# A windowed attention with a routed mixture of experts: root, scatters and copies in another order

## The chip, the cores and the metric

The kernel runs on one core of one Trainium2 chip. The metric is device time in microseconds (us). An execution that the hardware profiler recorded gives the profile page and the trace; three other executions give the median.

The engines of the core are named as the profile names them: PE is TensorE (PEld are its weight loads), DVE is VectorE, ACT is ScalarE, POOL is GpSimd, and SP is SyncE, which only issues transfers here.

## The reference

The inputs are q, k, v of shape (4, 8, 768, 64), eight expert vectors, and the two weight arrays of eight experts. All is float32.

```python
scores = scale * np.matmul(q, k.transpose(0, 1, 3, 2))
is_global = pos[None, :] < n_global                      # 8
is_local = (rel >= 0) & (rel < n_local)                  # 96
scores = np.where(keep, scores + bias, -1e9)             # bias: -slope of the head * distance
a = softmax(scores)
x = (a @ v) laid out as (3072, 512)

xn = x / (norm(x) + 1e-6);  en = expert_emb / (norm(expert_emb) + 1e-6)
logits = xn @ en.T / tau
expert_idx = np.argmax(logits, axis=1)
gate_w = softmax(logits)[arange(N), expert_idx]
for e in range(E):                                       # 8 experts, 512 -> 1024 -> 512
    h = np.maximum(x[mask] @ w1[e], 0.0)
    out[mask] = gate_w[mask, None] * (h @ w2[e])
```

## The kernel before

**The two stages.** The first stage (window_attention) computes attention and decides for each of the 3072 tokens which expert takes it. It writes the token's row to x_dram, and for each token a small record (its number twice and its gate) into a slot of its expert's list, meta, in device memory. The second stage reads the lists back, gathers each expert's rows, multiplies them by the expert's two weight matrices, and scatters the results to the output.

**The steps of the first stage.** A step handles two blocks of 96 queries, for four heads. A batch has two groups of heads (m = 0 and 1) and four steps (p) in each group, so there are 32 steps; in the last batch the two groups' steps are interleaved by halves. In step s TensorE first computes the scores of that step (score, L480: 64 short matmuls), then some transposes of coming queries and keys (turn, L455), then the router's matmuls and transposes for halves of a batch that are ready, and then the values' products of the step before (attend, L509 and L519). ScalarE takes the exponential of the scores (grow, L486) and VectorE multiplies it by a table of window and slope (weigh, L493). At every second step attend ends with copies out of PSUM: two xd copies (L524 on ScalarE; L525 on VectorE, from step 22 on ScalarE) and a copy or addition of the denominators, den (L530, L532, VectorE).

**The PSUM banks.** Five banks pa0 to pa4 go round for scores, transposes and router products. A bank is taken again when its reader (an exponential, a copy, a product) is done. Three further banks, od, hold the values' products; they are taken again once xd and den have been copied out.

**The router.** When a half of a batch (384 tokens) has its attention output, an object hf goes through phases, one a step: turn_x and store_x (L582, L591: the product of x with the reciprocal denominators, its store to x_dram, and on ScalarE its sum of squares, L596), turn_sums (L550, L553), score_experts (L559), turn_products (L568 to L574). Then the generator choose makes the decision, for a whole batch in the first two batches and for half a batch in the others. There are thus six routers. Its pieces, separated by yield, are: largest logit and one-hot choice (L203 to L211); the running counts by matmuls (L217, L220) and, on POOL, the root of the sums of squares (L224, a power of one half); adding the counts (L228, L230); then one piece with the reciprocal root and its product with the logits (L234, L235, L236, VectorE), the gate's exponential (L237, ScalarE), the slot number and the gate's sum (L240 to L250, VectorE). The last piece puts six or three scatters on a list, k.later.

**The scatters.** One scatter takes 128 tokens. VectorE writes the reciprocal gate into the record mt (L256), and POOL issues an indirect DMA of 128 records of 12 bytes to meta (L257). scatter_later takes the first one, two or three of the list in a step (one before step 24, two before step 29, three from there on), and makes each wait for the last score matmul of that step (scored). It stands before the router's turns of the step; in a step in which a router's phase equals hf.count, it stands behind them (L790 and L810).

**What sets the order.** On TensorE, ScalarE, VectorE and SP the order of the first stage is the order in which the program is written. POOL's order is chosen by the scheduler from what each instruction depends on. POOL has three kinds of work in the steps: copies of the values' first rows (v, L430), the roots (L224), and the scatters (L257). Late in the stage it also gathers the rows of expert 0's first 256 slots (first_gathers, L991), once these have been read back (L981). TensorE's products of those rows (first_turn, first_product, L663 and L671) follow the last step and stand beside the last router, its scatters, and the read of all lists (L1676).

**What calls the pieces.** half_turns sends the router on at phases 1 and hf.count; the loop's own lines send it on once more before attend; half_router, behind attend, sends it on to the large last piece when the phase is over hf.count. So the whole of L234 to L250 stands behind attend and its copies.

Of the kernel before, what the change touches and what calls it, by code (L numbers as in the profile page):

```python
# [12 lines left out]
ALU = mybir.AluOpType  # L13
# [178 lines left out]
def choose(k, b, i0, n, lg, ss, pool):  # L192


    nc, E = k.nc, k.E
    sl = slice(i0, i0 + n)
    lg, ss, eidx = lg[:, sl, :], ss[:, sl], k.eidx[:, 0:n, :]
# [23 lines left out]
                         rhs=oh[:, t : t + 1, :].to_broadcast([P, n - t, E]), start=False, stop=True,  # L221
                         skip_group_check=True)

    nc.gpsimd.tensor_tensor(out=ss, in0=ss, in1=k.half[:, 0:n], op=ALU.pow)  # L224

    yield
    both = new([n + 1, E], "both")
# [6 lines left out]
    nc.vector.tensor_scalar_add(ss, ss, 1e-6)  # L234
    nc.vector.reciprocal(out=ss, in_=ss)  # L235
    nc.vector.tensor_tensor(out=lg, in0=lg, in1=ss.unsqueeze(2).broadcast_to([P, n, E]), op=ALU.mult)  # L236
    nc.scalar.activation(lg, lg, AF.Exp)  # L237

    within = both[:, 0:n, :]
# [14 lines left out]
    def scatter(t, behind):  # L254

        nc.vector.reciprocal(out=mt[:, t : t + 1, 2], in_=gate[:, t : t + 1])  # L256
        i = nc.gpsimd.indirect_dma_start(  # L257
            out=k.meta[:], out_offset=bass.IndirectOffsetOnAxis(ap=slot[:, t : t + 1], axis=0),
            in_=mt[:, t, :], in_offset=None,
        )  # L260
        if behind:
            wait_for(k, i, [behind])

        if k.scatters:
            k.tc.declare_no_dep(i.ins, group="scatters", reason="slots are distinct")
        k.tc.add_to_no_dep_group("scatters", i.ins)
        k.scatters.append(i.ins)
# [28 lines left out]
def scatter_later(k, n, behind=None):  # L296

    for scatter, t in k.later[:n]:
        scatter(t, behind)
    del k.later[:n]  # L300


def route(k, b, xb, pool):

    nc, NT, E = k.nc, k.NT, k.E
    ss = pool.tile([P, NT], F32, name="ss", tag="ss")
    for t in range(NT):
        sq = pool.tile([P, k.DM], F32, name="sq", tag="sq")
        nc.scalar.activation(sq[:], xb[:, t, :], AF.Square, accum_out=ss[:, t : t + 1])
    lg = pool.tile([P, NT, E], F32, name="lg", tag="lg")  # L310
    for t in range(NT):
        tp = k.work.tile([P, 512], F32, name="work", tag="work")
        for c in range(k.NC):
            nc.tensor.transpose(tp[:, c * P : (c + 1) * P], xb[:, t, c * P : (c + 1) * P], k.ident[:])
        xt = pool.tile([P, k.NC, P], F32, name="xt", tag="xt")
        nc.scalar.copy(out=xt[:].rearrange("p c n -> p (c n)"), in_=tp[:])
        lp = k.work.tile([P, 512], F32, name="work", tag="work")
        for c in range(k.NC):
            nc.tensor.matmul(lp[:, 0:E], lhsT=xt[:, c, :], rhs=k.en[:, c, :],
                             start=c == 0, stop=c == k.NC - 1)  # L320
        nc.vector.tensor_copy(out=lg[:, t, :], in_=lp[:, 0:E])
    steps = choose(k, b, 0, NT, lg, ss, pool)
    next(steps)
    steps.send(k.work.tile([P, 512], F32, name="work", tag="work"))
    next(steps)
    next(steps)

# [49 lines left out]
def window_attention(k, ctx):  # L377
# [25 lines left out]
    def bank():  # L403
        turn_of[0] += 1
        return banks[turn_of[0] % len(banks)]
# [191 lines left out]

    def start_half(t, h):
        hf = Net()
        hf.t, hf.h, hf.phase = t, h, 0  # L600
        late = t.b >= B - 2

        hf.count = 2 if late else 3
        hf.router = choose(k, t.b, 3 * h if late else 0, 3 if late else NT, t.lg, t.ss, rt_p) if late or h else None
        return hf
# [10 lines left out]
    def half_turns(hf):  # L616
# [12 lines left out]
        if hf.router and hf.phase == hf.count:  # L629
            hf.router.send(k.free)  # L630

    def half_router(hf):

        if hf.router and hf.phase > hf.count:
            next(hf.router)
        if hf.phase == hf.count + 1 and hf.h == 1 and hf.t.b < B - 2:
            check_sums(hf.t)
        if (hf.t.b, hf.h, hf.phase) == (B - 2, 1, 3):
            first_base()
# [110 lines left out]
        for s, x in zip(at, pieces):  # L750
            turns[s].append(x)

    waiting, active = [], []
    weights = [(0, i) for i in range(PIECES)]
    for s, (g, p) in enumerate(steps):
        if s % 8 == 0:
# [29 lines left out]
        grow(us[0], 0)  # L786
        grow(us[0], 1)
        weigh(us[0])
        due = 1 if s < len(steps) - 8 else 2 if s < len(steps) - 3 else 3
        if not any(hf.router and hf.phase == hf.count for hf in active):  # L790
            scatter_later(k, due, scored)
            due = 0
        grow(us[1], 0)
        todo = [(x.pairs[a], i) for x, a, i in turns[s]]
        if todo:
# [11 lines left out]
            weigh(us[1])  # L807
        for hf in active:
            half_turns(hf)
        scatter_later(k, due, scored)  # L810
        if s == len(steps) - 1:
            first_gathers()
        ready = s > 8 * (B - 1) - 2 and steps[s - 1][0].m == 1 and steps[s - 1][1] % 2
# [3 lines left out]
        for hf in active:  # L817
            if hf.router and hf.phase == hf.count:
                next(hf.router)
        if s > 0:  # L820
            q, qp = steps[s - 1]
            attend(q, qp, s < len(steps) - 10)
            if q.m == 1 and qp % 2:
                waiting.append((prev, qp // 2))
# [20 lines left out]
    hf = start_half(t, 1)  # L845
# [11 lines left out]
    k.weights = weights  # L857
    first_product(0)
    hf.router.send(bank()[:, 3 * P :])
    next(hf.router)  # L860
    next(hf.router)
    scatter_later(k, len(k.later))
# [403 lines left out]
def wait_for(k, i, others):  # L1266
    for x in others:
        k.tc.add_manual_dep(i.ins, x.name,
                            mybir.DependencyInfo(mybir.DependencyClass.Sync, mybir.DependencyReason.DATA),
                            reason="it comes behind all of them")  # L1270
# [509 lines left out]
```

## Time and profile before

| | us |
|---|---|
| three executions | 522.73, 523.97, 524.47 (median 523.97) |
| the profiled execution | 524.56 |
| its span, first to last instruction | 522.8 |
| TensorE busy | 500.1 (96%) |
| VectorE busy | 301.8 (58%) |
| ScalarE busy | 197.2 (38%) |
| POOL busy | 153.7 (29%) |
| indirect DMA of a scatter (L257), on POOL, mean, 24 of them | 1.13 |
| v copy (L430), mean, 15 of them | 1.24 |
| root (L224), median of six | 0.89 |
| L234, L236, L237, median | 0.16, 0.18, 0.22 |

A matmul's end is modelled, so a busy TensorE need not be one at its peak. Idle time of an engine that is not on the way to the end costs nothing. In a row of the timeline the figure in brackets is the time that the engine stood idle before it, and what ended that time; "issue" is time in which it waited for nothing that the profile shows.

### The profile page before, as it was taken

The numbers are of one execution on the slowest core, as the hardware profiler recorded it, in microseconds if no ns is written. First come the engines' busy times: TensorE is split into PE (matmuls) and PEld (weight loads), VectorE is DVE, ScalarE is ACT, GpSimd is POOL, SyncE is SP. The second block draws the span as 40 slices with busy tenths as digits, with TensorE's granted clock in tenths as the row PEclk, the third lists the DMA queues.
The fourth block names the chain that finished last, engine by engine and source line by source line (L and its number), as shares of the span: only waits on it lengthen the run. The fifth ranks groups of instructions, "written<-read, shape, count | busy, mean of one in ns | idle before, by whom it ended". The sixth has DMA issues, their size and how long they took to land.

```text
span 522.8 us, 13699 instructions
## 1 busy us (share of the span) xinstructions
PE 500.1 (96%) x5606; PEld 411.3 (79%) x5606; DVE 301.8 (58%) x602; ACT 197.2 (38%) x493; POOL 153.7 (29%) x169
## 2 busy tenths in 40 slices
PE   7899999999988998999999999999999999999995
PEld 7677887887765787859878759989889789859964
DVE  5647667666685664756745606765646644715531
ACT  4867766766653411302322312412312222302210
POOL 4221121442544235354240024144053050013023
PEclk9999999999998999999999999999999999999999
DMA  9999998898443346817573018357056064001001
GB/s 169 200 188 181 220 261 207 212 229 177 104 103 92 94 102 118 265 56 287 195 284 118 2 44 296 150 197 263 3 217 242 4 224 163 1 16 67 0 22 67
DMA packets 111421, 76.32 MB, mean 146 GB/s; under 512 B 87077, under 2 KB 95269, under 8 KB 111281
## 3 DMA queue, kind: packets, MB, share of 16 engines
q1 hardware_dynamic: 102769, 59.00, 42.1%
q0 software_dynamic: 6912, 15.26, 8.8%
q8 instruction: 63, 1.03, 0.9%
q14 instruction: 77, 0.63, 0.4%
q10 hardware_dynamic: 1600, 0.39, 0.3%
HBM read 61.66 MB, written 17.16 MB: 151 GB/s over the span
## 4 chain that ended last, share of the span: by engine, by line
PE 67%; issue 18%; DVE 3%; POOL 3%; ACT 3%; DMA 3%; SPq 1%; POOLq 1%; ACTq 0%; DVEq 0%
PE big L1303 17%; PE big L1108 9%; PE od L509 7%; PE pa L480 5%; PE work L1236 4%; PE od L519 3%; PE pa L455 3%; PE work L1108 3%; PE work L1249 3%; PE pa L671 2%; PE work L1017 2%; POOL out_dram L1255 2%; PE big L1279 2%; PE pa L582 2%; PE work L1027 1%
## 5 line engine op out<-in xcount | busy, mean ns | idle before, releaser
L493 DVE TENSOR_TENSOR ex<-ex,table 126x768 f32<-126x768 f32 x64 | 61.3, 964 | 45.1 <-ACT ex L486 44.9
L1315 DVE TENSOR_TENSOR hT<-big,hT 128x320 f32<-128x320 f32 (+4 forms) x70 | 39.4, 566 | 49.9 <-PE big L1303 49.7
L1255 POOL DMA_INDIRECT out_dram<-y_arm,tids x17 | 17.1, 1004 | 167.4 <-ACT y_arm L1238 121.1
L486 ACT ACTIVATE ex<-pa 126x384 f32<-126x384 f32 (+1 forms) x128 | 53.3, 477 | 24.4 <-PE pa L480 18.6
L1303 PE MATMUL big<-xT,w1t 128*128 128x160 f32 (+4 forms) x336 | 59.4, 330 | 1.1 <-issue 1.1
L1303 PEld LDWEIGHTS big<-xT,w1t 128*128 128x128 f32 x336 | 54.2, 190 | 3.9 <-issue 2.0
L991 POOL DMA_INDIRECT xg<-x_dram,idss x32 | 35.4, 1106 | 42.9 <-PE big L1303 21.5
L509 PE MATMUL od<-ex,v 126*64 126x192 f32 (+1 forms) x576 | 47.0, 309 | 0.0
L480 PE MATMUL pa<-qT,kT 64*32 64x128 f32 (+4 forms) x2048 | 41.0, 263 | 3.7 <-issue 3.5
L480 PEld LDWEIGHTS pa<-qT,kT 64*32 64x32 f32 (+1 forms) x2048 | 30.2, 105 | 16.7 <-issue 12.3
L257 POOL DMA_INDIRECT meta<-mt,slot x24 | 27.2, 1133 | 49.9 <-DVE rd L553 20.9
L509 PEld LDWEIGHTS od<-ex,v 126*64 126x64 f32 x576 | 35.3, 139 | 7.9 <-issue 3.8
L1303 PE MATMUL big<-xsum,fsum 128*128 128x160 f32 (+4 forms) x224 | 39.6, 330 | 0.0
L1020 ACT COPY xT<-work 128x256 f32<-128x256 f32 x56 | 18.1, 375 | 56.0 <-PE work L1017 55.3
L1303 PEld LDWEIGHTS big<-xsum,fsum 128*128 128x128 f32 x224 | 36.1, 190 | 1.2
L1236 PE MATMUL work<-w2t,hT 128*128 128x512 f32 x80 | 35.1, 594 | 0.0
L1108 PE MATMUL big<-wsum,hsum 128*128 128x256 f32 x136 | 31.1, 380 | 1.1 <-issue 0.6
L1317 ACT ACTIVATE hT<-hT 128x320 f32<-128x320 f32 (+4 forms) x42 | 21.6, 533 | 25.5 <-DVE hT L1315 25.3
L430 POOL COPY v<-v 30x896 f32<-30x896 f32 (+1 forms) x15 | 18.4, 1239 | 41.1 <-DMA v<-in_v_dram 28.9
L1108 PEld LDWEIGHTS big<-wsum,hsum 128*128 128x128 f32 x136 | 25.7, 190 | 5.6 <-issue 1.4
L1236 PEld LDWEIGHTS work<-w2t,hT 128*128 128x128 f32 x80 | 15.1, 190 | 17.7 <-issue 17.6
L1113 DVE TENSOR_TENSOR ptmp<-big,ptmp 128x256 f32<-128x256 f32 x16 | 6.7, 421 | 38.0 <-PE big L1108 20.0
(246 smaller groups left out, 899.8 us busy)
## 6 DMA issues: line engine op xcount, KB each, us to landing
w1t<-in_moe_w_dram SPq DMA_DIRECT2D x6, 2048.0 KB
w2t<-in_moe_w_dram SPq DMA_DIRECT2D x6, 2048.0 KB
v<-in_v_dram SPq DMA_DIRECT2D x32, 192.0 KB
x_dram<-xs SPq DMA_DIRECT2D x23, 256.0 KB
k<-in_k_dram SPq DMA_DIRECT2D x28, 192.0 KB
q<-in_q_dram SPq DMA_DIRECT2D x28, 192.0 KB
w1t<-in_moe_w_dram SPq DMA_DIRECT2D x32, 128.0 KB
w2t<-in_moe_w_dram SPq DMA_DIRECT2D x32, 128.0 KB
```

What stands on the lines that cost most here:

```text
L257: i = nc.gpsimd.indirect_dma_start(out=k.meta[:], out_offset=bass.IndirectOffsetOnAxis(ap=slot[:, t : t + 1], axis=0), in_=mt[:, t, :], in ...
L480: i = nc.tensor.matmul(u.sp[e][k0:k1, a * n + c0 : a * n + c1], lhsT=t.kT[rows, j, k0:k1], rhs=t.qT[rows, j * BLK + c0 : j * BLK + c1], st ...
L486: nc.scalar.activation(u.ex[:, e], u.sp[e][0:ROWS, 0 : 2 * u.n].rearrange("p (a c) -> p a c", a=2), AF.Exp, scale=k.scale)
L493: nc.vector.tensor_tensor(out=exv, in0=exv, in1=tab[:, :, 0 : u.n // BLK, :], op=ALU.mult)
L509: nc.tensor.matmul(g.od[a][e * D : (e + 1) * D, at : at + c1 - c0], lhsT=g.v[0:ROWS, 2 * a + e, u.j, :], rhs=u.ex[:, e, a, c0:c1], start=f ...
L991: i = k.nc.gpsimd.indirect_dma_start(out=xg[:], out_offset=None, in_=k.x_dram[0 : upto or k.N + 1, :], in_offset=bass.IndirectOffsetOnAxis ...
L1108: i = self.k.nc.tensor.matmul(ps, lhsT=x[:, f, :], rhs=w[:, f, :], start=f == 0 and not add, stop=True, skip_group_check=True)
L1236: nc.tensor.matmul(ps[:], lhsT=hT[:, f, j * P : (j + 1) * P], rhs=w2[:, f, :], start=i == 0, stop=i == k.NF - 1)
L1255: i = k.nc.gpsimd.indirect_dma_start(out=k.out.rearrange("t (i m) -> (t i) m", i=n), out_offset=bass.IndirectOffsetOnAxis(ap=ids, axis=0), ...
L1303: nc.tensor.matmul(to[f // 2][:, f % 2 * 256 : f % 2 * 256 + h], lhsT=x[:, l, f * P : (f + 1) * P], rhs=y[:, l, 0:h], start=not (add or f ...
L1315: nc.vector.tensor_tensor(out=to, in0=x, in1=z, op=ALU.add)
L1317: nc.scalar.activation(to, to, AF.Relu)
```

## The change

1. choose keeps its root instruction in k.root, and scatter_later makes every scatter that it issues in a step wait for that root as well as for scored.
2. scatter_later stands in one place in every step, before the second unit's exponentials and the router's turns; the second place and its condition are gone.
3. The router's last piece is cut in two by a yield behind L236. A new function half_root sends the router through the first part (L234 to L236, VectorE) ahead of attend. The second part, with the gate's exponential on ScalarE, stays behind attend.

In choose:

```diff
-    nc.gpsimd.tensor_tensor(out=ss, in0=ss, in1=k.half[:, 0:n], op=ALU.pow)
+    k.root = [nc.gpsimd.tensor_tensor(out=ss, in0=ss, in1=k.half[:, 0:n], op=ALU.pow).ins]
...
     nc.vector.tensor_tensor(out=lg, in0=lg, in1=ss.unsqueeze(2).broadcast_to([P, n, E]), op=ALU.mult)
+
+    yield
     nc.scalar.activation(lg, lg, AF.Exp)
...
         if behind:
-            wait_for(k, i, [behind])
+            wait_for(k, i, behind)
```

In window_attention (and one more next(...) where a router is run to its end at once):

```diff
-        hf.t, hf.h, hf.phase = t, h, 0
+        hf.t, hf.h, hf.phase, hf.rooted = t, h, 0, False
...
+    def half_root(hf):
+
+        if hf.router and hf.phase > hf.count and not hf.rooted:
+            next(hf.router)
+            hf.rooted = True
+
     def half_router(hf):
 
+        half_root(hf)
         if hf.router and hf.phase > hf.count:
             next(hf.router)
...
-    waiting, active = [], []
+    waiting, active, k.root = [], [], []
...
-        due = 1 if s < len(steps) - 8 else 2 if s < len(steps) - 3 else 3
-        if not any(hf.router and hf.phase == hf.count for hf in active):
-            scatter_later(k, due, scored)
-            due = 0
+        scatter_later(k, 1 if s < len(steps) - 8 else 2 if s < len(steps) - 3 else 3, [scored] + k.root)
         grow(us[1], 0)
...
         for hf in active:
             half_turns(hf)
-        scatter_later(k, due, scored)
...
         for hf in active:
             if hf.router and hf.phase == hf.count:
                 next(hf.router)
+        for hf in active:
+            half_root(hf)
         if s > 0:
             q, qp = steps[s - 1]
             attend(q, qp, s < len(steps) - 10)
```

More of the change, by code (lines that the diff above doesn't have):

```diff
@@ L324, in route @@
     steps.send(k.work.tile([P, 512], F32, name="work", tag="work"))
+    next(steps)
     next(steps)
@@ L859, in window_attention @@
     hf.router.send(bank()[:, 3 * P :])
+    next(hf.router)
     next(hf.router)
```

## The prediction

> **What bounds the kernel now.** I read the page first: spans by engine, then the chain that ended last, then the timeline in order of time.
>
> ```profile
> span 522.8 us, 13699 instructions
> PE 500.1 (96%) x5606; PEld 411.3 (79%) x5606; DVE 301.8 (58%) x602; ACT 197.2 (38%) x493; POOL 153.7 (29%) x169
> ...
> PE 67%; issue 18%; DVE 3%; POOL 3%; ACT 3%; DMA 3%; SPq 1%; POOLq 1%; ACTq 0%; DVEq 0%
> ```
>
> TensorE carries the end; the change touches only the 32 attention steps (to about 184 us), and everything behind hangs on their end: last root (183.56), last scatters (187.18 to 191.42), slots read back (195.71), gathers (199.96). So a microsecond of TensorE there should be worth one at the end, if it is TensorE that waits. Timeline, step 14 to 15 (start us, duration us, what, count, [idle before <- releaser]):
>
> ```profile
> 79.67 0.55 DVE L525 COPY xd<-od 128x384 f32<-128x384 f32 x1
> ...
> 80.13 0.55 DVE L532 TENSOR_TENSOR den<-od,den 128x384 f32<-128x384 f32 x1
> 80.60 0.16 DVE L234 TENSOR_SCALAR ss<-ss 128x6 f32<-128x6 f32 x1
> ...
> 81.26 0.24 ACT L237 ACTIVATE lg<-lg 128x48 f32<-128x48 f32 x1 [1.75 <-DVE lg L236]
> ...
> 81.41 1.07 ACT L486 ACTIVATE ex<-pa 126x384 f32<-126x384 f32 x3
> ...
> 81.94 0.55 PE L455 MATMUL pa<-ident,k 128*128 128x128 f32 x3 [0.51 <-ACT ex L486]
> ```
>
> The router's three small operations stand behind two copies; ScalarE's gate exponential waits for them, the score exponentials queue behind it, and TensorE misses a bank: 0.51 us lost. Step 22 to 23 loses 0.34 in the same way, step 28 to 29 loses 1.18 (L550).
>
> The same view, step 25 to 26:
>
> ```profile
> 136.88 0.21 DVE L256 RECIPROCAL mt<-gate 128x1 f32<-128x1 f32 x2
> ...
> 137.83 1.05 POOL L257 DMA_INDIRECT meta<-mt,slot  x1 [0.41 <-issue]
> 137.97 0.87 PE L480 MATMUL pa<-qT,kT 64*32 64x128 f32 x40
> 139.11 0.43 PE L480 MATMUL pa<-qT,kT 64*32 64x128 f32 x5 [0.27 <-issue]
> 139.18 0.96 POOL L257 DMA_INDIRECT meta<-mt,slot  x1 [0.30 <-issue]
> 139.84 0.44 PE L480 MATMUL pa<-qT,kT 64*30 64x96 f32 x5 [0.29 <-issue]
> 140.59 0.48 PE L480 MATMUL pa<-qT,kT 64*32 64x128 f32 x14 [0.31 <-issue]
> ```
>
> A step's 64 score matmuls take 1.13 us nearly everywhere. Where a second indirect DMA in a row falls on them they crawl, waiting for nothing shown: 3.10 in step 26, 1.86 in 29, 3.84 in 30, 2.60 in 31 (here gathers), an excess of 1.97 + 0.73 + 2.71 + 1.47 = 6.9 us. A single scatter on them (steps 16, 17, 24, 27) costs nothing. Some 32 to 40 matmuls pass first; the crawl ends about 0.5 us after the last of the DMAs. After step 30, TensorE having been busy 2.95 of 4.26 us, its clock is halved:
>
> ```profile
> 159.16:163.42 4.26, 2.95 (x72) 1.83 (x69) 0.00 (x0) 1.43 (x6) 2.06 (x3) 1.00 0.32 97
> 163.42:166.83 3.41, 3.41 (x33) 2.51 (x35) 3.12 (x10) 1.69 (x6) 0.19 (x1) 0.50 0.17 44
> ```
>
> (columns: stretch, length, busy PE, PEld, DVE, ACT, POOL, granted clock, DMA). So when scatters start matters more than any busy time.
>
> **What the Trainium skill says.** "Perfetto Trace Analysis", Sequencer Loop: an engine's instructions are queued and wait there for their semaphores. The trace agrees: L486 behind L237 above. "DMA: Bandwidth & Descriptors", Anatomy of one DMA, SWDGE path: about 2 us fixed, most of it the write receipt. Here a v copy that waits for a scatter went 2.7 us after that scatter's start (129.71 to 132.41), another 4.8 (96.22 to 101.01); I use 2.7 to 5.8 (108.42, released 114.2). "TensorE: Matmul & The Clock Gate", part 1: the clock follows recent activity and is full or half; the 0.50 above agrees. No page I used says that indirect DMAs slow TensorE's issue; that is the trace alone.
>
> **The change, part by part.** Sums are against the profiled 524.56 us (span 522.8 and 1.8 around it), 0.6 over the median 523.97. In the changed order TensorE, ScalarE and SP keep their sequences; VectorE and POOL don't.
>
> (a) Chain L234 to L236 ahead of L525/L530/L532, in four routers (steps 14, 22, 26, 28). The chain is 0.55 us (80.60 to 81.15), so copies are 0.55 later. Step 14: xd 80.22, den 80.68 to 81.23; TensorE needs them at 82.3 (L582, L550), covered by about 1 us; uncovered it costs 0.55. The gate exponential goes at 80.33 instead of 81.26, the score ones at 80.58, when scores exist (0.75 after 79.83). Gain 0.51; step 22, likewise, 0.34. Sum 0.85.
>
> (b) Steps 25 and 27: mt's reciprocals ahead of x's products. Step 25: they go at 134.89 (end of L493) instead of 136.88, so the two scatters at 135.84 (0.74 behind, as now) to 138.15 instead of 137.83 to 140.14; the crawl would reach 138.6, 0.6 us into step 26's scores. Gain 1.97 - 0.6 = 1.37.
>
> (c) The cost of (b): POOL's order now has these scatters ahead of the second v copy, which waits for their landing, and ahead of the root (L224). Scatter two starts at 137.1; landing 139.8 to 142.9; v copy (0.93 to 1.66) and root (0.89) end at 141.6 to 145.5. VectorE's chain in step 26 reaches it at 144.7 (L493's end, 146.07, less 1.37). Stall 0 to 0.8; I take 0.2, hidden because den then ends at about 146.0 and the od banks are wanted at 146.2 (147.58 less 1.37). Later than that, den, the banks and L509 are late one for one.
>
> (d) Steps 27 to 29. Step 27's scatters follow reciprocals at 147.5 and end near 151.0, before step 29's scores at 151.13 (152.50 less 1.37). Root 151.84, chain to 152.4, den to 152.95, gate exponential 152.5, score exponentials 152.65 instead of 154.23. L550 goes at 153.15 instead of 154.76 (156.13 less 1.37): gain 1.6, which holds the 0.73 crawl and most of the 1.18 wait. The chain's wait for the root (about 1.2 us at the head of VectorE's queue) delays den and the second weighing; both are still there when asked for.
>
> (e) Step 30. VectorE gains no more than 1.4 here, so reciprocals go at 156.0, three scatters at 156.94 to 160.4, the x products end at 157.2. TensorE's scores start at 156.2, wait for that bank until 157.2, end 157.8, mostly ahead of the crawl (before: 163.0 less 1.37 = 161.6). Beyond (d) a gain of 2.2; the crawl then meets L509, with a quarter of the issue rate: minus 0.6.
>
> (f) Step 31: gathers at 165.4 to 168.4 (5.0 behind the scatters, as 161.83 to 166.84 now); scores at 162.5 are ahead of them: plus 1.47, minus 1.2 for the dense attention matmuls that then stand under them: 0.27.
>
> (g) The new dependence itself: POOL is in order, so five scatters get one more check behind a root long past. No row shows it; spacing of first scatters behind their reciprocals (0.3 to 0.8) bounds it at 0 to 0.5 us each, on POOL, which idles; 0 taken.
>
> Sum: 0.85 + 1.37 + 1.6 + 2.2 - 0.6 + 0.27 = 5.7. The half clock costs about 1.6 (L509 2.19 for 1.20, L568 and L519 0.6); I don't count its going, since TensorE still has gaps. 523.97 - 5.7, with 0.3 for (c): 518.6.
>
> **Rivals.** *Crawl not avoided* (20%): its cause is the position in TensorE's stream, or scatters crawl wherever they lie. For it: step 31's has gathers, not scatters. Against: 28 other steps. Left are (a) and about 0.8 of step 29's wait: 1.65, so 522.3. *Given back* (13%): earlier scores only meet the next late thing, VectorE (5.30 busy of 6.66 us in step 29) or the landing before the gathers: 523.9. *Slower* (15%): the root behind the v copy behind the landing. If the scatters don't get ahead (still 139.18), landing 145.0, copy 146.6, root 147.5, against 146.0 wanted: VectorE's head stalls 1.5 us, den, gate exponential, score exponentials and od banks with it, some 2.5 through step 28 against 0.85 gained: 525.6. It decides once the landing comes later than about 5.4 us behind the second scatter's start (144.7 less 0.89 less 1.3, less 137.1) by more than the gains. *Change without effect* is part of "given back": the dependence alone moves two scatters.
>
> **How the numbers follow.** Main case 52%, 516.2 (half clock gone, no loss in (e)) to 520.8 (one crawl back). Faster: 0.52 + 0.12 of the first rival = 0.64; same, within 0.3% or 1.6 us (what a measurement here can tell): 0.08 + 0.11 = 0.19; slower 0.02 + 0.15 = 0.17. The range leaves out the main case's best tenth (0.05) and what lies above 524.3, nearly all of the slower rival and the top of "given back" (0.15): 516.3 to 524.3.
>
> **What would show it.** L237 right behind the copies, without 1.75 idle; L455 in step 15 without 0.51; score groups of 1.13 in steps 26, 29, 30, with scatters ended before or started late in them; the v copy between step 25's scatters and the root, and VectorE's wait for the root under 1 us in step 26. Wrong: crawls of 2 to 4 us still there beside scatters, or L234 waiting longer for the root than TensorE gains.

## The result and the profile after

The changed kernel took 524.04 us (median of 20 executions, 519.86 to 530.44), and the kernel before, run in the same batch, 526.41 us (20 executions). Ratios, here and below, leave out the few slow executions, those more than 1.5% above the shortest of the same kernel (one here). The ratio is 0.9948, with a 95% interval of 0.9927 to 0.9969: 2.7 us less (1.6 to 3.8), half of the forecast 5.4. Five later batches, each with its own runs of the kernel before, qualify this: in the three in which the changed kernel was run again the ratio was 0.998, 1.006 and 1.008. The traces below show where it gains; why it loses in two of the later batches they show in part.

The page of the profiled execution (523.85 us), span and busy time:

```profile
span 522.0 us, 13698 instructions
PE 500.9 (96%) x5606; PEld 412.8 (79%) x5606; DVE 301.3 (58%) x602; ACT 197.4 (38%) x493; POOL 148.7 (28%) x169
```

TensorE is as busy as before, and the span is 0.8 us shorter, less than the 2.7 us of the timed executions: the two profiles show where time moves, and do not add up to the measured gain. The averages do not show what happened; the steps do. The start of each step's first score matmul, after minus before, in us: step 24, -1.51; 26, -1.44; 27, -3.19; 28, -2.05; 30, -3.46; 31, -2.72; the first product behind the stage (179.81 instead of 181.53), -1.72. So 3.2 us are won by step 27, 1.1 are lost in step 27, 1.4 won again by step 30, and 1.7 given back between step 30 and that product. Another 0.9 us goes in the second stage, which these experiments did not follow.

**The early exponential.** The timeline of the kernel after, step 14 to 15 (start, duration, what, count, [idle before <- releaser]):

```profile
79.35 0.16 DVE L234 TENSOR_SCALAR ss<-ss 128x6 f32<-128x6 f32 x1
...
80.02 0.24 ACT L239 ACTIVATE lg<-lg 128x48 f32<-128x48 f32 x1 [0.83 <-DVE lg L236]
80.27 1.10 ACT L489 ACTIVATE ex<-pa 126x384 f32<-126x384 f32 x3
...
80.96 0.49 PE L458 MATMUL pa<-ident,k 128*128 128x128 f32 x3
```

The chain now stands ahead of the copies, the gate's exponential (L239, before L237) has waited 0.83 us instead of 1.75, the score exponentials follow at once, and the transpose (L458, before L455) no longer waits 0.51 us. Step 15 is 0.78 us shorter and step 23 0.62. But step 16 is 0.52 us longer: its scores now start 0.28 us behind the start of a scatter (84.71 and 84.43; before it was 1.06, 85.80 and 84.74), and take 1.64 us instead of 1.13. They do so in every profile with the early chain from a batch in which scores crawl (1.57 to 1.64 us), and in none with one scatter a step where the chain stays behind the copies (1.13).

**Step 26, and its price in step 27.** The same view, step 25 to 27:

```profile
134.27 0.98 POOL L259 DMA_INDIRECT meta<-mt,slot  x1 [0.28 <-POOL v L433]
135.55 1.66 POOL L259 DMA_INDIRECT meta<-mt,slot  x1 [0.30 <-DVE xs L594]
136.53 1.37 PE L483 MATMUL pa<-qT,kT 64*32 64x128 f32 x64
...
141.03 0.93 POOL L433 COPY v<-v 30x896 f32<-30x896 f32 x1 [3.82 <-issue]
142.04 0.92 POOL L224 TENSOR_TENSOR ss<-ss,half 128x3 f32<-128x3 f32 x1
143.43 0.16 DVE L234 TENSOR_SCALAR ss<-ss 128x3 f32<-128x3 f32 x1
143.94 0.55 DVE L533 COPY den<-od 128x384 f32<-128x384 f32 x1
144.54 0.40 PE L217 MATMUL od<-oh,prefix 128*128 128x24 f32 x2 [1.03 <-DVE lg L236]
```

The two scatters have ended 0.7 us into step 26's scores, which take 1.37 us instead of 3.10. But the v copy waits for their landing, the root for the v copy, the chain for the root, den stands behind the chain, and TensorE's first router matmul (L217) is written into the od bank that den has to empty: it waits 1.03 us, where it waited nothing before:

```profile
146.59 0.40 PE L217 MATMUL od<-oh,prefix 128*128 128x24 f32 x2
```

**Step 30, where the gain was to be largest:**

```profile
155.71 0.65 PE L483 MATMUL pa<-qT,kT 64*32 64x128 f32 x32
156.22 0.96 POOL L259 DMA_INDIRECT meta<-mt,slot  x1 [3.55 <-PE pa L562]
156.55 0.65 PE L483 MATMUL pa<-qT,kT 64*32 64x128 f32 x21 [0.19 <-DVE xs L594]
157.48 0.96 POOL L259 DMA_INDIRECT meta<-mt,slot  x1 [0.30 <-issue]
157.55 0.41 PE L483 MATMUL pa<-qT,kT 64*32 64x128 f32 x4 [0.35 <-issue]
```

The scatters came 0.7 us earlier than forecast, and the second bank of the scores 0.6 us earlier too. But the crawl does not wait for the second scatter: the gap of 0.35 us opens at 157.20, the second scatter starts at 157.48. It catches the last eleven matmuls, and the group takes 3.67 us (3.83 before). Step 31's scores then start with the gathers (165.26 and 165.22) and take 3.33 us instead of 2.60.

### The profile page after: what moved, and what is told of

Same layout as the page of the kernel before. It is cut to its first block, busy times and chain, and to the rows that moved or that the text cites. A ratio compares the mean times of both kernels' runs of the same rounds, so it can differ in the third digit from the quotient of the medians.

```text
span 522.0 us, 13698 instructions
## 1 busy us (share of the span) xinstructions
PE 500.9 (96%) x5606; PEld 412.8 (79%) x5606; DVE 301.3 (58%) x602; ACT 197.4 (38%) x493; POOL 148.7 (28%) x169
## 3 DMA queue, kind: packets, MB, share of 16 engines
q8 instruction: 63, 1.03, 0.9%
## 4 chain that ended last, share of the span: by engine, by line
PE 64%; issue 24%; POOL 5%; DVE 3%; ACT 2%; POOLq 1%; DMA 1%; DVEq 0%
PE big L1312 15%; PE big L1117 8%; PE od L512 7%; PE pa L483 6%; PE pa L458 4%; PE work L1258 3%; PE od L522 3%; PE pa L681 3%; PE work L1117 3%; POOL out_dram L1264 3%; PE work L1245 3%; PE work L1026 2%; PE big L1288 2%; PE pa L585 2%; PE work L1036 1%
## 5 line engine op out<-in xcount | busy, mean ns | idle before, releaser
L512 PE MATMUL od<-ex,v 126*64 126x192 f32 (+1 forms) x576 | 46.8, 309 | 0.0
L1000 POOL DMA_INDIRECT xg<-x_dram,idss x32 | 32.3, 1011 | 43.9 <-PE big L1312 21.7
L483 PE MATMUL pa<-qT,kT 64*32 64x128 f32 (+3 forms) x2048 | 40.8, 268 | 2.8 <-issue 2.5
L512 PEld LDWEIGHTS od<-ex,v 126*64 126x64 f32 x576 | 35.2, 138 | 7.7 <-issue 3.5
L433 POOL COPY v<-v 30x896 f32<-30x896 f32 (+1 forms) x15 | 16.6, 1119 | 49.0 <-DMA v<-in_v_dram 30.5
```

Of the source, the lines that this page charges most:

```text
L483: i = nc.tensor.matmul(u.sp[e][k0:k1, a * n + c0 : a * n + c1], lhsT=t.kT[rows, j, k0:k1], rhs=t.qT[rows, j * BLK + c0 : j * BLK + c1], st ...
L512: nc.tensor.matmul(g.od[a][e * D : (e + 1) * D, at : at + c1 - c0], lhsT=g.v[0:ROWS, 2 * a + e, u.j, :], rhs=u.ex[:, e, a, c0:c1], start=f ...
L1000: i = k.nc.gpsimd.indirect_dma_start(out=xg[:], out_offset=None, in_=k.x_dram[0 : upto or k.N + 1, :], in_offset=bass.IndirectOffsetOnAxis ...
```

## The experiments

Two statements stood against each other at first. *Crawl*: the gain is that scatters leave the scores, and what is missing from the forecast are L217's wait and the crawls that remain in steps 30 and 31. *Order alone*: VectorE's order makes the gain, and the scatters' place is neutral. Each batch ran on one chip, between runs of the kernel before; ratios are to those. "Excess" is the time of the score groups of steps 24 to 31 above 1.13 us each, in the profiled execution. "Half clock" is worked out for every execution from its mean granted clock c as 2 (1 - c) times its span, and given as a mean over the executions that the ratio uses. Executions of one kernel differ by up to 2%, so a single profile shows which wait stands where, and not what it is worth in the median.

### First batch: the parts alone, and two repairs (before: 523.63 us)

**The chain's part alone** (changed kernel, with the scatters' two places and their wait as before):

```diff
-        scatter_later(k, 1 if s < len(steps) - 8 else 2 if s < len(steps) - 3 else 3, [scored] + k.root)
+        due = 1 if s < len(steps) - 8 else 2 if s < len(steps) - 3 else 3
+        if not any(hf.router and hf.phase == hf.count for hf in active):
+            scatter_later(k, due, [scored])
+            due = 0
...
         for hf in active:
             half_turns(hf)
+        scatter_later(k, due, [scored])
```

> The chain L234 to L236 ahead of attend alone; the scatters and their wait as in the kernel before. Theory (crawl): the exponentials come earlier in steps 14, 22, 26 and 28 (0.5 + 0.3 + up to 1.2 us), but the scatters of step 25 and 29 still fall on the next step's scores, so step 26's 64 score matmuls stay near 3.1 us; about -1 us, ratio 0.998. Rival (order alone): VectorE's order makes the whole gain and the scatters' place is neutral; about -2.7 us, ratio 0.995.

Measured: 524.69 us, ratio 1.0022 (0.9999 to 1.0045). Neither number came. *Order alone* is out. The earlier exponentials are there, but so is the crawl: step 26's scores are clean this time (1.13, the scatters started 0.92 us behind the first of them), and the scatters of step 27 start at 149.65 and 150.93, on step 28's scores (149.04), which take 3.74 us instead of 1.12. Excess 6.68 us, against 6.87 in the first profile of the kernel before. In this profile, moving the chain had only moved the crawl. Why the forecast gain did not come in the timed executions is not shown beyond that.

**The scatters' part alone** (changed kernel, the chain behind the copies again):

```diff
-        for hf in active:
-            half_root(hf)
         if s > 0:
             q, qp = steps[s - 1]
             attend(q, qp, s < len(steps) - 10)
```

> The scatters' place and their wait for the root alone; the chain stays behind the copies as in the kernel before. Theory (crawl): step 26's scores 1.1 to 1.5 us instead of 3.1, step 29's near 1.1 to 1.9; the exponential waits of steps 15, 23 and 29 stay; about -1.5 us, ratio 0.997. Rival (order alone): step 26's scores may shorten, but the time goes to the next wait; ratio 1.000.

Measured: 522.10 us, ratio 0.9982 (0.9962 to 1.0003). Step 26 1.51 us, step 29 1.39, step 30 3.82, step 31 1.65; excess 3.83. L217 waits 0.67. The score groups are as *crawl* had them. The time alone does not decide: the interval holds both the 0.997 of *crawl* and the 1.000 of its rival. But in the same batch this part ran 2.0 us shorter than the chain's part (0.8 to 3.1).

**One chain behind den** (changed kernel, the chain behind the copies for one router):

```diff
         for hf in active:
-            half_root(hf)
+            if (hf.t.b, hf.h) != (B - 2, 0):
+                half_root(hf)
```

> The changed kernel, but in the router of step 26 the chain stays behind den's addition, as before; only VectorE's order differs, in one place. Theory: L217's wait of 1.03 us for den in step 27 goes, and step 28's score group starts about 1 us earlier than in the changed kernel; about -1 us against the changed kernel, ratio 0.993 to the kernel before. Rival: the gate's exponential comes later instead and the bank that it holds up costs the same; step 28 starts where it does in the changed kernel, ratio 0.995.

Measured: 521.41 us, ratio 0.9966 (0.9943 to 0.9988). L217's wait falls to 0.40 us, and step 27 takes 4.55 us instead of 5.18. But step 29 then takes 5.90 us instead of 5.18: from step 27's start to step 30's it is 13.95 us here and 13.91 in the changed kernel. The wait was real, and in this profile its removal was given back within two steps. In the sum the rival was right, though not in the place: step 28 did start earlier, and step 29 took the time back, by what is not shown. The profiled execution was one of the longest (525.12 us, median 521.41).

**The last three scatters later** (changed kernel, nothing taken from the list in step 29):

```diff
-        scatter_later(k, 1 if s < len(steps) - 8 else 2 if s < len(steps) - 3 else 3, [scored] + k.root)
+        if s != len(steps) - 3:
+            scatter_later(k, 1 if s < len(steps) - 8 else 2 if s < len(steps) - 3 else 3, [scored] + k.root)
...
-        if s == len(steps) - 3:
+        if s == len(steps) - 2:
             scatter_later(k, len(k.later))
             first_rows()
```

> The changed kernel, but no scatters in step 29: the three go behind step 30's scores, and the lists' first rows are read one step later. Theory (crawl): step 30's 64 score matmuls take 1.1 to 1.6 us instead of 3.67, and the crawl then meets dense attention matmuls or nothing; -1.5 to -3 us against the changed kernel, ratio 0.990 to 0.992. The gathers come about 3 us later, which is hidden unless stage two's first rows are then late. Rival (position): step 30's scores crawl wherever the scatters are, 3.5 us or more, and the time is that of the changed kernel, 0.995, or more by what the gathers are late.

Measured: 525.74 us, ratio 1.0042 (1.0020 to 1.0064). Step 30's scores take 1.30 us, as expected of *crawl*; but the three scatters (161.57 to 165.05) meet step 31's (162.50), which take 4.30 us. The half clock is 8.1 us in the mean, against 3.1 in the kernel before. The crawl is not tied to a step; nor is it easily got rid of.

### Second batch: the same kernel again, a spread that did not come about, and a direct test of the crawl (before: 527.11 us)

The changed kernel once more:

> The changed kernel once more, to stand beside the others on one chip. Both theories: 0.995 to the kernel before, as measured; step 30's scores near 3.7 us, step 31's near 3.3, L217's wait for den near 1.0 us. If the two parts alone (1.002 and 0.998) add up, it is 1.000 instead.

Measured: 527.22 us, ratio 0.9977 (0.9952 to 1.0002). Steps 30 and 31 as expected (3.69, 3.60), but L217 waits 2.25 us, twice as long: the first v copy went at 137.05 instead of 133.06.

Two attempts to spread the last three scatters over three steps, the second with the one chain behind den:

```diff
-        scatter_later(k, 1 if s < len(steps) - 8 else 2 if s < len(steps) - 3 else 3, [scored] + k.root)
+        scatter_later(k, 1 if s < len(steps) - 8 or s > len(steps) - 3 else 2, [scored] + k.root)
+        if s == len(steps) - 1:
+            first_rows()
...
         if s == len(steps) - 3:
-            scatter_later(k, len(k.later))
-            first_rows()
+            scatter_later(k, 1)
```

> The changed kernel, but the three scatters of the end of step 29 are spread: one there, one behind step 30's scores, one behind step 31's, and the lists' first rows are read behind the third. Theory (crawl needs two indirect DMAs in a row on the scores): step 30's group 1.1 to 1.6 us instead of 3.7, step 31's 1.1 to 1.7 instead of 3.3, no gathers under it; the half clock at 161 gone or later; -2.5 to -4 us against the changed kernel, ratio about 0.989. Rival (late steps crawl whatever lies there): step 30 or 31 still over 3 us, ratio 0.995 or more. What the spread costs: the gathers about 4 us later, which shows only if their transposes are then late.

> The same spread, and in step 26 the chain behind den's addition. Theory: the wait of L217 for den (1.03 us) goes too; ratio 0.987, the shortest of all. Rival: the two gains overlap, the earlier scores only wait for the next thing; ratio that of the spread alone.

Measured: 529.43 us, 1.0020 (0.9987 to 1.0053), and 526.77 us, 0.9995 (0.9972 to 1.0017). The edit did not do what it was for: step 29 still took all three off the list, and they ran in a row at 159.42, 160.69 and 161.95 in the second kernel. So step 30 crawled (3.85 and 3.72). What did change is that the gathers came later, and step 31's scores took 1.13 us in both: the gathers are what made that step crawl. No time was won: against the changed kernel of this batch the first took 2.2 us more (0.9 to 3.5) and the second as much.

**The crawl by itself** (kernel before):

```diff
-        due = 1 if s < len(steps) - 8 else 2 if s < len(steps) - 3 else 3
+        due = 3
```

> The kernel before, but up to three scatters in every step from the first router on. Theory (crawl comes from a second and third indirect DMA in a row under the scores, wherever they are): score groups of steps 16 to 18 that took 1.12 us with one scatter take 2 to 4 us. Rival (late steps only): 1.13 us there.

Measured, one execution: 531.97 us, against a median of 527.11. Steps 16, 17 and 24 take 3.72, 3.19 and 3.73 us where one scatter left them at 1.12 or 1.13. The timeline of this kernel, step 16:

```profile
86.41 1.41 PE L480 MATMUL pa<-qT,kT 64*32 64x128 f32 x40
86.82 0.97 POOL L257 DMA_INDIRECT meta<-mt,slot  x1 [0.30 <-issue]
88.10 0.96 POOL L257 DMA_INDIRECT meta<-mt,slot  x1 [0.30 <-issue]
88.15 0.42 PE L480 MATMUL pa<-qT,kT 64*32 64x128 f32 x4 [0.33 <-issue]
```

The same picture as in step 26 of the kernel before, ten steps earlier: several indirect DMAs in a row on the scores make the crawl, in whatever step. This is shown, for a batch that crawls. Step 20 bears it out where nobody aimed at it: in five kernels of the first, second and fifth batch two scatters, the first held back by a v copy, ran in a row on its scores, which took 2.69 to 3.55 us. In the third and fourth batch the same pair left them at 1.21 to 1.30.

### Third batch: the reciprocals at once, and one scatter a step (before: 519.40 us)

> The changed kernel a third time, as the partner of the others on this chip. Theory: 0.995 to 0.998 to the kernel before, the two values measured; the crawl of steps 30 and 31 near 3.7 and 3.3 us.

Measured: 522.12 us, ratio 1.0057 (1.0036 to 1.0078): slower than before, and outside what was expected. Steps 30 and 31 are clean (1.12 and 1.13 us). L217 waits 2.28 us.

Reciprocals at once (changed kernel), alone and with two scatters in step 29 and one in step 30:

```diff
     def scatter(t, behind):
-        nc.vector.reciprocal(out=mt[:, t : t + 1, 2], in_=gate[:, t : t + 1])
         i = nc.gpsimd.indirect_dma_start(
...
+    nc.vector.reciprocal(out=mt[:, :, 2], in_=gate)
     if k.scatters is None:
-        nc.vector.reciprocal(out=mt[:, :, 2], in_=gate)
```

> The changed kernel, but a router takes all its reciprocal gates in one instruction behind its gate's sum, and the scatters wait for scores and root alone. Theory (the scatters crawl on the next step's scores because their reciprocals stand late in VectorE's queue): scatters of steps 25 to 28 start within 0.5 us of the end of their own step's scores and stand under the dense attention matmuls; steps 26 to 29 all 1.13 us; step 30 still 2 to 3 us, since step 29's router is itself late; -1 to -2 us against the changed kernel. Rival (the crawl only moves to whatever runs beside the scatters): L512 and L522 or the transposes grow by as much; no change.

> The reciprocals at once, and two scatters in step 29 and one in step 30 with the first rows read behind it. Theory: no score group over 2 us from step 24 to 30, the gathers about 2 us later than in the changed kernel, the shortest of all: ratio about 0.988. Rival: as for the two edits alone, 0.995 or more.

Measured: 520.84 us, 1.0033 (1.0012 to 1.0053), and 520.29 us, 1.0026 (1.0006 to 1.0047). Excess 0.21 and 0.30 us: clean, but in this batch the changed kernel has next to none either (1.26, of which 0.78 in step 28 under the half clock). L217 waits 0.67 and 0.84. Both are shorter than the changed kernel (by 1.6 and 1.9 us in the mean, give or take 1.0) and longer than the kernel before.

One scatter a step from step 29, the first rows read in step 31:

```diff
-        scatter_later(k, 1 if s < len(steps) - 8 else 2 if s < len(steps) - 3 else 3, [scored] + k.root)
+        scatter_later(k, 1 if s < len(steps) - 8 or s > len(steps) - 4 else 2, [scored] + k.root)
+        if s == len(steps) - 1:
+            first_rows()
...
-        if s == len(steps) - 3:
-            scatter_later(k, len(k.later))
-            first_rows()
```

> The changed kernel, but from step 29 on one scatter in a step instead of three, and the lists' first rows are read behind the third, in step 31. Theory: step 30's scores 1.1 to 1.9 us instead of 3.7, step 31's 1.13 since the gathers come later; -2 to -3.5 us against the changed kernel up to step 31, and at the end as much less what the gathers then cost elsewhere. Rival: step 30 crawls with one scatter too, or the gathers' crawl comes back under the last step's matmuls; no change or slower.

Measured, six executions: 526.39 us, 1.0126 (1.0080 to 1.0172). The scatters were spread this time (160.35, 164.31, 169.10), and the gathers came at 176.0: the first product starts at 183.68 instead of 178.65 in the changed kernel of this batch. The half clock is 15.9 us in the mean, against 4.7 in the kernel before. What the spread costs was the larger part. The kernel before was not profiled in this batch.

### Fourth batch: why it is slower where nothing crawls (before: 518.81 us)

> The kernel before, unchanged, profiled on this chip beside the others. If the crawl is a property of the kernel: steps 26, 29, 30 and 31 near 3.1, 1.9, 3.8 and 2.6 us as in the first profile. If it differs by chip or batch, these groups differ by over 1 us, in the same direction as those of the changed kernel here.

Measured: 517.60 us in one execution; score groups 24 to 31 all 1.12 or 1.13 us. Step 30 is the clean comparison, for the scatters lie at the same places. First the first profile of the kernel before, then this one:

```profile
158.34 0.96 POOL L257 DMA_INDIRECT meta<-mt,slot  x1 [2.50 <-DVE rd L553]
159.17 0.86 PE L480 MATMUL pa<-qT,kT 64*32 64x128 f32 x39
159.60 0.96 POOL L257 DMA_INDIRECT meta<-mt,slot  x1 [0.30 <-issue]
160.34 0.44 PE L480 MATMUL pa<-qT,kT 64*32 64x128 f32 x6 [0.31 <-issue]
```

```profile
155.53 0.95 POOL L257 DMA_INDIRECT meta<-mt,slot  x1 [2.35 <-DVE rd L553]
156.36 1.13 PE L480 MATMUL pa<-qT,kT 64*32 64x128 f32 x64
156.79 0.96 POOL L257 DMA_INDIRECT meta<-mt,slot  x1 [0.30 <-issue]
```

The same program, scatters 0.83 us before and 0.43 us behind the first score in both: 3.83 us in one batch, 1.13 in the other. The crawl is no fixed property of the kernel. Nor of the chip: this batch ran on the chip of the second, in which groups did crawl. Across batches the kernel before takes 523.6 to 527.1 us where profiles show the crawl (the result's, first, second and fifth; in the first, second and fifth these are profiles of other versions), and 518.8 and 519.4 where they don't.

> The changed kernel, the partner of the next two. Where step 25's first v copy goes before 134 us, L217 waits about 1.0 us and the ratio is near 0.995; where it goes after 136 us, L217 waits about 2.3 us, and the ratio is 1.000 or more.

Measured: 522.18 us, ratio 1.0079 (1.0048 to 1.0109), with the wait expected for a late copy. Timeline of the changed kernel here, and the view by stretches (stretch, length, busy PE, PEld, DVE, ACT, POOL, granted clock, DMA share, GB/s):

```profile
137.04 0.93 POOL L433 COPY v<-v 30x896 f32<-30x896 f32 x1 [6.28 <-DMA x_dram<-xs]
...
143.91 1.15 POOL L433 COPY v<-v 30x896 f32<-30x896 f32 x1 [2.31 <-issue]
145.14 0.88 POOL L224 TENSOR_TENSOR ss<-ss,half 128x3 f32<-128x3 f32 x1
146.06 0.17 DVE L234 TENSOR_SCALAR ss<-ss 128x3 f32<-128x3 f32 x1 [1.80 <-POOL ss L224]
...
147.18 0.40 PE L217 MATMUL od<-oh,prefix 128*128 128x24 f32 x2 [2.28 <-DVE den L533]
```

```profile
145.65:149.06 3.41, 1.88 (x20) 1.77 (x22) 2.83 (x13) 1.75 (x5) 1.42 (x2) 1.00 0.25 59
149.06:152.48 3.42, 3.42 (x76) 2.34 (x74) 1.92 (x5) 1.99 (x6) 2.54 (x3) 0.51 0.38 79
```

The first v copy goes at 137.04 (133.06 in the result's profile); the two scatters stand behind it on POOL, then the second v copy with its wait for the landing, then the root. VectorE waits 1.80 us at L234, den comes behind, and L217 waits 2.28. TensorE is busy for 1.88 of 3.41 us, and for the next 3.41 its clock is halved. Against the kernel before in the same batch, step 27 takes 6.84 us instead of 4.04 and step 28 4.59 instead of 3.47; step 29 wins back 1.32. The profiled span is 519.1 instead of 515.9.

**The root ahead of the v copy** (changed kernel; the second v copy of the last group waits for the root, so POOL does scatter, scatter, root, copy), alone and with the earlier and split scatters of the third batch:

```diff
+        def spread_v():
+            return nc.gpsimd.tensor_copy(out=g.v[BLK:ROWS, h0:h1, 1:], in_=g.v[BLK:ROWS, h0:h1, 0:1].to_broadcast([GLB, h1 - h0, NB - 1, D]))
+        if (g.b, g.m, h0) == (B - 1, 1, 2):
+            k.spread_v = spread_v
+        else:
+            spread_v()
...
             half_turns(hf)
+        if s == len(steps) - 6:
+            wait_for(k, k.spread_v(), k.root)
```

> The changed kernel, but the second v copy of the last group waits for the root of step 26's router, so that POOL does two scatters, root, v copy instead of two scatters, v copy, root; nothing else differs in order. Theory (the root behind the copy behind the landing): VectorE no longer waits at L234, den follows at once, L217 waits 0.4 to 1.0 us instead of up to 2.3; -1 to -2 us against the changed kernel where the copies are late, 0 to -0.5 where they are early. Rival (the loss lies in the half clock or in the chain standing ahead of den, not in POOL): L217's wait as long as before, no change in time.

> The same, with all reciprocal gates at once and two scatters in step 29 and one in step 30 (first rows behind it). Theory: both gains add, no score group over 2 us from step 24 to 30 and L217 below 1 us: -3 us against the changed kernel, shorter than both kernels, 0.992 to 0.997. Rival: the earlier scores meet the half clock, as in the earlier batches; the time of root_first or more.

Measured: 521.51 us, 1.0053 (1.0032 to 1.0075), and 521.90 us, 1.0048 (1.0026 to 1.0070). Timeline of the first:

```profile
138.60 1.29 POOL L224 TENSOR_TENSOR ss<-ss,half 128x3 f32<-128x3 f32 x1
142.55 0.16 DVE L234 TENSOR_SCALAR ss<-ss 128x3 f32<-128x3 f32 x1
...
143.66 0.40 PE L217 MATMUL od<-oh,prefix 128*128 128x24 f32 x2 [0.40 <-DVE den L539]
```

VectorE no longer waits, L217 waits 0.40, step 27 takes 4.54 us, no half clock follows in these steps, and the profiled span is 515.2. The first v copy was in between in this execution (134.67), but the root ended at 139.89, 2.7 us before L234 wanted it: the root behind the copy was the cause of the wait, and this is shown. In the timed executions it gives back a third of the loss; set directly against the changed kernel it is 1.7 us shorter (0.4 to 3.1), as expected. The profiled execution was the shortest of 22 (517.02 us, median 521.51), so it does not show where the rest is lost. That rest goes with the half clock, 7.6 us in the mean instead of 4.5; an execution's time grows by 0.47 us per us of half clock, which makes 1.4 of the 2.7 us. Which waits bring it in those executions, one profile can't say, and what makes the remainder stays open. In the second kernel L217 still waited 1.19 us and step 27 took 6.66: its gains did not add.

### Fifth batch: the two parts again (before: 524.92 us)

> The scatters' place and wait alone, again (0.998 in the first batch, in which the scores crawled). Theory (the scatters' part brings the root behind the v copy, and the gain is the crawl alone): in a batch without crawl slower than before, 1.003 to 1.006, with L217 waiting 0.7 to 2 us; in one with crawl 0.998 again. Rival (the chain's part costs): 1.000 in a batch without crawl.

Measured: 523.34 us, 0.9966 (0.9944 to 0.9989). This batch crawls (step 30 3.85 us), and the scatters' part gains in it, this time clear of the noise. Its excess is 3.73 us; that of the next kernel, whose late scatters are those of the kernel before, 5.41.

The chain ahead for the first two routers alone (the first kernel of the first batch, with a condition):

```diff
         for hf in active:
-            half_root(hf)
+            if hf.t.b < B - 2:
+                half_root(hf)
```

> The chain ahead of attend for the routers of steps 14 and 22 alone; the scatters, and the two later routers, as in the kernel before. Theory: the exponentials' waits of steps 15 and 23 go (0.51 and 0.34 us), nothing else moves: -0.85 us, ratio 0.998, with or without crawl. Rival (earlier steps change when the transfers of the last batch meet the scores, or the clock): 1.000 or more.

Measured: 524.21 us, 0.9977 (0.9953 to 1.0001). Step 15 takes 5.19 us instead of 5.97 and step 23 5.19 instead of 5.80 (against the first profile of before), and step 16 5.66 instead of 5.20, with scores of 1.59; L217 does not wait; steps 26, 29 and 30 crawl as before (3.07, 1.87, 3.82). The expected 0.85 us are inside the interval, and so is nothing at all.

In the batches without crawl the kernel before is the shortest of all that ran. Where the scores crawl, the scatters' part alone (0.9982 and 0.9966), the change (0.9948 and 0.9977) and the change with one chain behind den (0.9966) can't be told apart. The scatters' part was not tried in a batch without crawl.

## Why the prediction was right in its direction and wrong in its size

In the result's batch the direction was right. In two later batches it was not, so the batch had its share in that.

- **(a) Chain ahead of the copies: right, but its price was missing.** The waits of steps 15 and 23 went, 0.51 and 0.34 us. "A single scatter on them (steps 16, 17, 24, 27) costs nothing" was misread: in steps 17, 24 and 27 that scatter had ended before the first score (90.67 and 91.00, 124.92 and 124.97, 144.39 and 144.99), and in step 16 the scores started 1.06 us behind its start. Moved 0.78 us ahead, step 16's scores met it and lost 0.51. Steps 15, 16 and 23 together gain 0.88, close to the forecast 0.85 by luck; the rest of the 1.51 by which step 24 starts earlier lies before step 14 and in steps 20 and 21.
- **(b) Step 25's scatters ahead of step 26's scores: right.** Step 26 gains 1.75 us instead of 1.37. It needs a batch that crawls, which the prediction took for granted.
- **(c) The price of (b): the step that failed first.** The order on POOL was as foreseen (scatter, scatter, landing, copy, root), but "hidden because ... the od banks are wanted at 146.2" named the wrong customer. L217 is written into an od bank ahead of L509, and wanted it at 143.5. So 1.03 us were lost, not 0.3. And the scatters' start was worked out from VectorE's reciprocals alone; they also stand behind the first v copy, which went at 136.1 to 137.1 in the changed kernel of three later batches. The root then ended at 145.7 to 146.4, past the bound of 145.5. That is the rival called *Slower*, with its mechanism, but with another landing: the one behind the moved scatters came in time (the copy went 3.97 us behind the second scatter's start in the fourth batch, 5.48 in the result's), while the first v copy waits for the landing of step 24's second scatter (by its semaphore in the traces, whatever transfer the row names). It went 4.9 us behind that scatter's start in the result's profile and 7.0 to 7.3 in the three later ones, where the prediction used 2.7 to 5.8.
- **(d) Step 29: right.** 1.13 us instead of 1.86, the transpose's wait 0.43 instead of 1.18 us. The chain's wait for the root, 1.70 us instead of 1.2, was covered there as stated.
- **(e) Step 30: wrong, and the largest part of what is missing.** A gain of 2.2 on the scores was forecast and 0.16 came; with the rest of the step it was 1.6 forecast against 0.74 lost. The step that failed is "mostly ahead of the crawl". It counted on the crawl from the second scatter on; with scores ending at 157.8 and that scatter at about 158.2 there was little room. In the trace the crawl began 1.0 us behind the first scatter, as a single one also slowed step 16, and it needs only the last eleven of 64 matmuls to cost as much as before. "VectorE gains no more than 1.4 here" was short as well: the reciprocals came 2.1 us earlier, and the scatters with them. Step 30 as a whole even grew by 0.74 us (9.55 instead of 8.81): the crawl went on into the transposes behind the scores, and the half clock of 161.3 stood over the products.
- **(f) Step 31: wrong.** The scores were to be ahead of the gathers; they started together, and took 0.73 us more than before. The gathers came 5.5 us behind the scatters, about as forecast (5.0); the scores were late because step 30 was.
- **(g) The new dependence: right.** No scatter is seen to be late by it: two start 0.3 us behind the root (143.25, 151.64), the first ones of the other groups 0.7 us behind their reciprocals (146.99, 156.22), as before (137.83).
- **The half clock: its going was not counted, and it did not go.** That it could grow was not counted either: 4.7 us in the mean before and 8.4 after in the third batch, 4.5 and 8.1 in the fourth. The Trainium skill ("TensorE: Matmul & The Clock Gate", part 1, what's actually happening) gives windows of about 3.4 us, and the half rate after an idle one. The stretches above agree in the length, 3.41 us; but the 3.41 us ahead of the half clock were not idle, TensorE being busy for 1.88 of them.

In the two profiles of the result the sum by steps is: 1.44 won before step 26 (0.85 of it (a)), 1.75 won in step 26 (b), 1.14 lost in step 27 (c), 1.41 won in steps 28 and 29 (d), 0.74 lost in step 30 (e), 1.00 lost from step 31 to the first product, 0.73 of it on step 31's scores (f): 1.72 us, where 5.4 was forecast. Short of the forecast are above all (e) by 2.3 us, (f) by 1.3 and (c) by 0.8. The premise below the sum, that the kernel before loses 6.9 us to crawling scores, was seen to hold in the result's batch and to fail in the fourth; by the other versions' profiles it held in the first, second and fifth and failed in the third. Where it fails, (b), (e) and (f) have nothing to win, and the price of (c) remains.

## What to carry to other kernels

A loss for which the trace shows no releaser may be one of that batch: profile the unchanged kernel in a second batch before you count on its removal. When a DMA is moved ahead of other work on an in-order engine, follow every instruction behind it down to the last engine that wants the result, and take its start from what stands ahead of it on that engine, not from its operands alone. When a bank is said to be covered, look for its first writer in the engine's order, not for its main one.

## What the runs showed of the hardware

- Two or three indirect DMAs in a row on POOL, or two gathers, slow a run of short matmuls to about five per 0.73 us, with idle stretches in which TensorE waits for nothing shown. A single one that starts 0.28 us ahead of the run cost it 0.5 us (step 16). Longer attention matmuls under a pair hardly slowed (step 24's pair at 126.93 to 129.15 in the changed kernel: L512 1.20 us, as elsewhere; L522 behind it 1.69 instead of 1.51). In two of six batches the same DMAs at the same places slowed next to nothing, on a chip that showed it in another batch. What differs was not found: the page's counts of packets and bytes are the same, instruction fetches included (63 and 77 packets). How the DMAs slow TensorE's issue is open too.
- Half clock starts on a fixed grid: within each trace its starts lie whole multiples of 3.413 us apart (161.31 and 519.71 us in the changed kernel: 105 of them). A wait of 2.28 us was followed by 3.41 us or more of half clock in all three profiles of the third and fourth batch that had it, and one of 1.68 us in the second batch was too; another there, of 2.25 us (145.30 to 147.55), was not. It lies across a line of that trace's grid (146.57), which fits, but was not tested.
- The landing that a POOL instruction waits for varies: the first v copy, which waits for step 24's second scatter, went 2.7 us behind its start in the first profile of the kernel before, and 7.3 us behind it in the changed kernel of the fourth batch.
